# Sparse attention and a maxout layer in one kernel: the list of work units in another order

## The chip, the core and the metric

The kernel runs on one core of one Trainium2 chip. The metric is device time in microseconds. Three runs of the kernel before gave 179.69, 180.04 and 180.06 us, a median of 180.04. One execution was also taken by the hardware profiler; all rows below are from it.

A core has a matrix engine (PE in the profile, its weight loads PEld), a vector engine (DVE), an activation engine (ACT), a general engine (POOL, also called GpSimd) and a queue that issues most transfers (SP). Each takes its own instructions strictly in the order in which they were written; an instruction that has to wait holds up everything behind it on its engine.

## The reference

```python
def _attn_ref(q, k, v, n_global, n_local):          # q, k, v: (4, 8, 768, 64), n_global 8, n_local 96
    scores = scale * np.matmul(q, k.transpose(0, 1, 3, 2))
    rel = pos[:, None] - pos[None, :]
    is_global = pos[None, :] < int(n_global)
    is_local = (rel >= 0) & (rel < int(n_local))
    keep = is_global | is_local
    dist = np.where(is_global & ~is_local, float(n_local), np.abs(rel).astype(np.float32))
    scores = np.where(keep, scores - slopes * dist, -1000000000.0)   # slopes: one per head
    a = softmax(scores)
    return np.matmul(a, v)
...
    x = attn_out.transpose(0, 2, 1, 3).reshape(B * S, H * D)         # (3072, 512)
    h = np.maximum(np.maximum(x @ w1, x @ w2), x @ w3)               # (3072, 768)
    return (h @ w_out)                                               # (3072, 512)
```

Each query sees the first 8 keys of its batch and the last 96 keys up to itself. All inputs are float32 in memory; the kernel multiplies in bfloat16.

## The kernel before

The 3072 tokens are 24 tiles T of 128 tokens, six to a batch. A tile's scores need its own keys, those of the tile before it, and the 8 global keys, which are written over the first 8 key columns of the tile before. The feed-forward part takes the tiles in seven chunks of 4, 2, 2, 4, 4, 4, 4 tiles.

The order of all work is written by hand, as the string SCHEDULE (line 25). Each word is a unit: a letter, its indices, and mostly a last number that picks the engine (0 ACT, 1 DVE, 2 POOL). Line 475 emits the units in the order of the string. Which instruction stands behind which is thus set by the string alone, on every engine and on SP.

The units, by letter:

- **l**, **c**, **x**: the first 12 tiles' q and k come in five groups. `l` loads one part of a group (line 158), `c` casts it to bfloat16 (183), `x` transposes it on PE (239) and copies the result from PSUM (243). In `l2.0` and `l2.1` the parts are q and k of the third group, tiles 4 and 5. Ending 4 in `x` splits the copy between ACT and DVE.
- **L**, **C n.0**, **X**: the same for single tiles from tile 12 on; `X` with ending 4 has a transfer on SP do the transposing (250), with other endings PE (261). **v** loads a tile's values (174), **C n.1** casts them (189).
- **S** scores of four heads and their exponential (283, 288). With ending 1 two more matmuls add the bias (275); otherwise **M** multiplies by a mask afterwards on DVE (307). **K** and **B** prepare masks (300) and biases (295).
- **G** and **V** write the global keys and values into place (214, 216, 221).
- **A** the weighted sum of values (322, 325), then reciprocal and product on DVE (331, 332). **T** transposes the result into the chunk's input: on PE with a copy (349, 350), or with ending 4 by a transfer on SP (340).
- **w**, **W** load and cast w1 to w3 (417, 427); **o**, **Q** the same for w_out (422, 430).
- **F c.f.j** one block of 128 hidden columns of chunk c with weight matrix j: four matmuls (361); j = 0 is copied to SBUF by ACT (366), j = 1 and 2 are maxima on DVE (368, 370). **O** is the product with w_out for a tile (376), its copy (382) and its store (383). **E** is the last chunk's O.
- **D** multiplies zeros on PE (436).

PSUM is tight: the scores and the weighted sums share two buffers, sp0 and sp1 (for `A` the last number picks one); F, O and some transposes share three; one more is for transposes. The raw q/k tiles have five buffers, the raw v tiles six.

Of the kernel before, what the change touches and what calls it, by code (L numbers as in the profile page):

```python
# [22 lines left out]


SCHEDULE = """
    K0 K1 K2 K3 K4 K5 l1.0 l1.1 D0.3 c0.0.2 B0.1 B1.1 B2.1 B3.0 K6 B4.1 B5.1 c0.1.1 c1.0.2 x0.0.4 B6.1
    B7.1 x0.1.4 S0.0.1 v0 l2.0 l2.1 K7 S0.1.1 G0.0 S1.0.1 S1.1.0 x1.0.3 c1.1.2 M0.0 M0.1 M1.0 v1 x1.1.4
    C0.1.2 v2 A0.1 G1.2 S2.0.1 M1.1 c2.0.2 x2.0.1 C1.1.1 S2.1.0 G2.2 S3.0.1 M2.0 M2.1 C2.1.1 T0.1 S3.1.1
    M3.0 M3.1 c2.1.2 v3 A1.0 C3.1.0 w0.0 V1.2 x2.1.2 w1.0 A2.1 V2.2 A3.0 T1.0 T2.1 T3.1 W1.0.1 W0.0.0
    G3.2 S4.0.0 S4.1.0 F0.0.0 F0.1.0 M4.0 F0.2.0 F0.3.0 G4.1 S5.0.0 M4.1 S5.1.0 w0.1 W0.1.1 w0.2 W0.2.2  # L30
    V3.2 F0.0.1 F0.1.1 F0.0.2 F0.1.2 v4 C4.1.0 A4.0 V4.2 w1.1 W1.1.2 W2.0.0 F0.4.0 F0.5.0 M5.0 M5.1 w1.2
    W1.2.2 v5 W2.1.0 T4.0 F0.2.1 F0.3.1 l3.0 l3.2 F0.4.1 l3.1 c3.0.2 c3.2.2 F0.5.1 o2 C5.1.0 A5.1 l3.3
    F0.2.2 Q2.2 F0.3.2 W2.2.0 o0 T5.0 F0.4.2 o1 F0.5.2 x3.0.0 F1.0.0 F1.1.0 c3.1.1 F1.2.0 x3.2.0 Q0.2
    F1.0.1 F1.1.1 F1.2.1 l4.0 l4.1 c3.3.0 F1.0.2 F1.1.2 F1.2.2 x3.1.2 x3.3.1 F1.3.0 F1.4.0 Q1.2 F1.3.1
    S6.0.0 S6.1.0 v6 v7 v8 G6.0 F1.3.2 F1.5.0 v9 c4.0.1 F1.4.1 S7.0.0 S7.1.0 G7.2 v10 M6.0 M6.1 M7.0
    M7.1 O0.0.0 F1.4.2 c4.1.1 C6.1.2 C7.1.2 L12 F1.5.1 S8.0.0 S8.1.0 x4.0.0 O0.1.0 A6.0 x4.1.2 A7.1 V7.2
    F1.5.2 v11 T6.0 O0.2.0 T7.1 G8.2 C8.1.2 S9.0.0 S9.1.0 G9.1 v12 v13 O0.3.0 F2.0.0 F2.1.0 S10.0.0 M8.0
    M8.1 M9.0 M9.1 S10.1.0 C9.1.2 L13 L14 F2.0.1 F2.1.1 F2.0.2 A8.0 C12.0.1 F2.1.2 G10.2 O1.0.0 V8.2
    A9.1 X12.1 M10.0 M10.1 C10.1.0 C11.1.0 F2.2.0 S11.0.0 S11.1.0 M11.0 M11.1 L15 F2.3.0 F2.4.0 O1.1.0
    V9.2 A10.1 F2.2.1 V10.2 T8.0 F2.3.1 F2.5.0 T9.0 A11.1 F2.4.1 T10.0 F2.2.2 F2.3.2 T11.1 F2.4.2  # L40
    S12.0.0 S12.1.0 F2.5.1 C13.0.2 C14.0.2 C15.0.1 X13.4 F3.0.0 F3.1.0 F3.0.1 G12.1 C12.1.0 F3.2.0
    F3.1.1 F3.2.1 S13.0.0 S13.1.0 F2.5.2 v14 C13.1.0 C14.1.2 M12.0 M12.1 F3.0.2 F3.1.2 X14.4 F3.2.2
    X15.4 G13.2 M13.0 M13.1 S14.0.0 S14.1.0 F3.3.0 F3.4.0 F3.5.0 M14.0 M14.1 G14.1 A12.0 A13.1 F3.3.1
    F3.4.1 F3.5.1 S15.0.0 M15.0 S15.1.0 G15.0 v15 V13.2 L16 L17 v16 T12.4 v17 M15.1 O2.0.0 C15.1.0 A14.0
    V14.2 F3.3.2 F3.4.2 T13.4 F3.5.2 C16.1.0 C16.0.2 X16.3 T14.4 C17.0.2 A15.1 X17.4 O2.1.0 S16.0.0
    S16.1.0 G16.1 L18 V15.2 L19 T15.1 M16.0 O3.0.0 M16.1 F4.0.0 F4.1.0 F4.0.1 F4.1.1 C18.0.2 L20 C19.0.2
    A16.1 F4.2.0 F4.3.0 S17.0.0 S17.1.0 F4.2.1 F4.0.2 F4.3.1 v18 M17.0 v19 M17.1 X18.3 X19.4 C20.0.0
    V16.2 F4.1.2 C17.1.2 O3.1.1 A17.1 F4.2.2 F4.3.2 S18.0.0 M18.0 S18.1.0 M18.1 F4.4.0 T16.4 T17.4
    F4.4.1 C18.1.2 C19.1.1 F4.4.2 X20.4 G18.1 S19.0.0 S19.1.0 F4.5.0 L21 M19.0 M19.1 v20 F4.5.1 A18.0
    T18.4 F4.5.2 A19.1 T19.4 V19.1 C21.0.1 X21.4 G19.1 L22 C22.0.2 L23 X22.4 O3.2.1 O3.3.0 O4.0.1  # L50
    S20.0.0 S20.1.0 M20.0 G20.0 O4.1.0 F5.0.0 F5.1.0 F5.2.0 S21.0.0 S21.1.0 G21.2 F5.0.1 F5.1.1 M20.1
    M21.0 F5.3.0 F5.0.2 F5.1.2 F5.2.1 F5.2.2 v21 C20.1.1 C21.1.2 F5.4.0 S22.0.0 M21.1 S22.1.0 C23.0.0
    F5.3.1 M22.0 M22.1 F5.5.0 F5.3.2 A20.0 V20.2 G22.2 v22 F5.4.1 X23.4 v23 F5.5.1 T20.4 A21.1 V21.1
    T21.4 F5.4.2 F5.5.2 S23.0.0 S23.1.0 M23.0 O4.2.0 M23.1 C22.1.2 A22.0 C23.1.0 O4.3.0 V22.2 T22.4
    A23.1 T23.4 O5.0.1 O5.1.0 O5.2.1 O5.3.0 F6.0.0 F6.1.0 F6.0.1 F6.0.2 F6.2.0 F6.3.0 F6.4.0 F6.1.1
    F6.2.1 F6.1.2 F6.3.1 F6.4.1 F6.2.2 F6.3.2 F6.5.0 F6.4.2 F6.5.1 F6.5.2 E
"""


# [1 line left out]
def kernel(  # L61
# [73 lines left out]
    xT = {}  # L135
# [87 lines left out]
    def early(T):  # L223
        return T < NSTART
# [109 lines left out]

    def u_XT(T, how):
        c, i = where[T]
        if i == 0:
            xT[c] = xT_pool.tile([128, NP, len(chunks[c]) * 128], BF16, name="xT", tag="xT")
        if how == 4:
            nc.sync.dma_start_transpose(out=xT[c][:, :, i * 128:(i + 1) * 128],  # L340
                                        in_=xb[T].rearrange("p h d -> p (h d)"))
            return
        if early(T):
            tp = psH.tile([128, NP, 128], BF16, name="xtp", tag="h")
        else:
# [4 lines left out]
        copies[how](xT[c][:, :, i * 128:(i + 1) * 128], tp)  # L350

    ht = {}
    h01s = {}

    def u_F1(c, f, j):
        W = len(chunks[c]) * 128
        if f == 0 and j == 0:
            ht[c] = ht_pool.tile([128, NF, W], BF16, name="ht", tag="ht")
        ps = psH.tile([128, W], FP32, name="h", tag="h")
        for dm in range(4):  # L360
            nc.tensor.matmul(ps, w123[f // 2][:, dm, j, (f % 2) * 128:(f % 2) * 128 + 128],  # L361
                             xT[c][:, dm], start=(dm == 0), stop=(dm == 3))
        if j == 0:
            h01 = h01_pool.tile([128, W], BF16, name="h01", tag="h01")
            h01s[c, f] = h01
            nc.scalar.copy(h01, ps)  # L366
        elif j == 1:
            nc.vector.tensor_max(h01s[c, f], h01s[c, f], ps)  # L368
        else:
            nc.vector.tensor_max(ht[c][:, f], h01s[c, f], ps)  # L370
# [58 lines left out]
    def cast_wo(i, how):  # L429
        copies[how](wo[:, 2 * i:2 * i + 2], wst["o", i])  # L430

    def u_D(i, n):

        wp = psH.tile([128, 512], FP32, name="wp", tag="h")
        for _ in range(n):
            nc.tensor.matmul(wp, zeros[:, 0:128], zeros, start=True, stop=True)

    with tc.manual_schedule():
# [71 lines left out]
```

## Time and profile before

| | |
|---|---|
| median of the runs | 180.04 us |
| profiled execution, first to last instruction (span) | 178.3 us |
| median less span | 1.74 us |
| PE busy | 166.9 us (94%) |
| DVE, ACT, POOL busy | 118.9, 103.1, 37.5 us |
| first matmul of the feed-forward part (F0.0.0) | 23.44 us after the span's start |
| last matmul ends | about 175.05 us |
| moved by transfers | 35.52 MB, mean 199 GB/s |

The page tells of the profiled execution only its span; its own run time is not listed, so the 1.74 us are taken as what lies around the span. Busy time of PE overlaps from one matmul to the next, so a full PE row says that it did not stand idle, and not that each matmul is as short as can be. A landing time below is the start of a transfer's issue on SP plus the time from issue to landing.

### The profile page before, as it was taken

The numbers are of one execution on the slowest core, as the hardware profiler recorded it, in microseconds if no ns is written. First come the engines' busy times: TensorE is split into PE (matmuls) and PEld (weight loads), VectorE is DVE, ScalarE is ACT, GpSimd is POOL, SyncE is SP. The second block draws the span as 40 slices with busy tenths as digits, with TensorE's granted clock in tenths as the row PEclk, the third lists the DMA queues.
The fourth block names the chain that finished last, engine by engine and source line by source line (L and its number), as shares of the span: only waits on it lengthen the run. The fifth ranks groups of instructions, "written<-read, shape, count | busy, mean of one in ns | idle before, by whom it ended". The sixth has DMA issues, their size and how long they took to land.

```text
span 178.3 us, 3960 instructions
## 1 busy us (share of the span) xinstructions
PE 166.9 (94%) x1529; PEld 95.8 (54%) x1551; DVE 118.9 (67%) x237; ACT 103.1 (58%) x160; POOL 37.5 (21%) x65
## 2 busy tenths in 40 slices
PE   3599799999999999999999999999999999999992
PEld 0455644558867677845555555545444555444442
DVE  4519875986787689748979447979358896136620
ACT  4867898646689858555744837351772643341122
POOL 4355203543343112310007024100020401000000
PEclk9999999999999999999999999999999999999998
DMA  5999999999998999989544999769889674610006
GB/s 140 292 271 242 357 320 384 320 361 358 251 193 213 229 254 236 174 171 233 94 90 118 159 247 235 157 132 186 173 153 294 136 143 146 224 42 4 0 11 226
DMA packets 83587, 35.52 MB, mean 199 GB/s; under 512 B 66160, under 2 KB 78320, under 8 KB 83568
## 3 DMA queue, kind: packets, MB, share of 16 engines
q1 hardware_dynamic: 83424, 35.20, 82.8%
q8 instruction: 12, 0.20, 0.5%
q10 hardware_dynamic: 144, 0.07, 0.1%
q14 instruction: 7, 0.06, 0.1%
HBM read 25.17 MB, written 6.29 MB: 176 GB/s over the span
## 4 chain that ended last, share of the span: by engine, by line
PE 85%; DMA 8%; SPq 2%; issue 1%; POOL 1%; DVE 1%; ACT 1%; ACTq 0%
PE h L361 53%; PE po L376 17%; PE sp L283 6%; DMA rawv<-in_v_dram 4%; DMA rawp<-in_q_dram 4%; PE op L322 3%; PE op L325 2%; SPq L174 2%; PE tpp L239 2%; PE xtp L349 1%; SPq L158 1%; POOL qkp L183 1%; PE tp L261 1%; DVE xb L332 0%; ACT va L189 0%
## 5 line engine op out<-in xcount | busy, mean ns | idle before, releaser
L361 PE MATMUL h<-xT,w 128*128 128x512 bf16 (+1 forms) x491 | 99.2, 348 | 0.7 <-issue 0.2
L361 PEld LDWEIGHTS <-w 128*128 128x128 bf16 x504 | 46.9, 98 | 40.5 <-DVE w L427 0.3
L288 ACT ACTIVATE P<-sp 128x1024 bf16<-128x1024 f32 (+1 forms) x48 | 43.4, 955 | 20.6 <-PE sp L283 20.4
L368 DVE TENSOR_TENSOR h<-h,h 128x512 bf16<-128x512 bf16 (+1 forms) x42 | 25.3, 610 | 25.7 <-PE h L361 16.5
L366 ACT CAST h<-h 128x512 bf16<-128x512 f32 (+1 forms) x42 | 21.6, 533 | 21.5 <-PE h L361 21.3
L376 PE MATMUL po<-wo,ht 128*128 128x512 bf16 (+2 forms) x147 | 33.1, 362 | 0.5
L370 DVE TENSOR_TENSOR ht<-h,h 128x512 bf16<-128x512 bf16 (+1 forms) x42 | 25.1, 607 | 3.7 <-PE h L361 3.0
L307 DVE TENSOR_TENSOR P<-P,wmask 128x1024 bf16<-128x1024 bf16 x36 | 24.8, 718 | 3.6 <-ACT P L288 3.5
L376 PEld LDWEIGHTS <-ht 128*128 128x128 bf16 x156 | 14.0, 98 | 13.9
L382 ACT COPY ost<-po 128x512 f32<-128x512 f32 (+2 forms) x20 | 11.2, 564 | 17.8 <-PE po L376 17.7
L332 DVE TENSOR_TENSOR xb<-op,rz 128x512 bf16<-128x512 f32 x24 | 16.6, 692 | 0.8
L283 PEld LDWEIGHTS <-qkT 64*128 64x128 bf16 x352 | 10.2, 96 | 10.0 <-issue 8.0
L283 PE MATMUL sp<-qkT 64*128 64x128 bf16 x352 | 15.2, 223 | 0.4 <-DVE xb L332 0.4
L322 PEld LDWEIGHTS <-P 128*128 128x128 bf16 x192 | 12.5, 97 | 2.5 <-ACT P L288 0.2
L221 POOL COPY va<-vaf 8x260 int32<-8x260 int32 x14 | 6.3, 452 | 34.5 <-PE op L325 34.5
L198 POOL CAST qkb<-raw 128x1024 bf16<-128x1024 f32 x7 | 7.2, 1037 | 27.7 <-DMA raw<-in_q_dram 18.9
L322 PE MATMUL op<-va,P 128*128 128x65 bf16 x160 | 12.3, 193 | 0.7 <-ACT va L189 0.6
L239 PE MATMUL tpp<-identb,qkp 128*128 128x128 bf16 x96 | 8.5, 246 | 4.0 <-POOL qkp L183 3.4
L325 PEld LDWEIGHTS <-P 128*128 128x128 bf16 x160 | 10.4, 97 | 2.2 <-issue 0.7
L239 PEld LDWEIGHTS <-qkp 128*128 128x128 bf16 x96 | 7.0, 111 | 5.8 <-POOL qkp L183 4.3
L325 PE MATMUL op<-va,P 128*128 128x65 bf16 x128 | 9.9, 193 | 0.0
L243 ACT COPY qkT<-tpp 128x1024 bf16<-128x1024 bf16 (+1 forms) x9 | 7.9, 874 | 3.4 <-PE tpp L239 3.4
(66 smaller groups left out, 107.5 us busy)
## 6 DMA issues: line engine op xcount, KB each, us to landing
rawv<-in_v_dram SPq DMA_DIRECT2D x24, 256.0 KB, 4.8
out_dram<-ost SPq DMA_DIRECT2D x23, 256.0 KB, 2.3
rawp<-in_q_dram SPq DMA_DIRECT2D x6, 512.0 KB, 7.2
rawp<-in_k_dram SPq DMA_DIRECT2D x6, 512.0 KB, 7.4
wst<-in_moe_w_dram SPq DMA_DIRECT2D x3, 1024.0 KB, 9.7
raw<-in_q_dram SPq DMA_DIRECT2D x12, 256.0 KB, 4.1
raw<-in_k_dram SPq DMA_DIRECT2D x12, 256.0 KB, 4.8
wst<-in_moe_w_dram SPq DMA_DIRECT2D x3, 512.0 KB, 8.7
```

Source lines behind the costliest of these rows:

```text
L239: nc.tensor.transpose(tp[:, e, j - lo], qb["p", n, s][:, e, 2 * j:2 * j + 2].rearrange("i h d -> i (h d)"), identb)
L283: nc.tensor.matmul(sp[:, hh, j2, ds], qT(T - ds, 1)[hsl, jp], qT(T, 0)[hsl, jp], start=not how, stop=True, skip_group_check=True)
L288: nc.scalar.activation(P[:, :, 0:n], sp.rearrange("p a b d n -> p (a b) d n")[:, :, 0:n], AF.Exp, bias=0.0, scale=scale)
L307: nc.vector.tensor_mul(P, P, wmask[:, g, :, 0:2])
L322: nc.tensor.matmul(o, P[:, i, 0], heads(va[T])[:, h], start=True, stop=(t == 0), skip_group_check=True)
L325: nc.tensor.matmul(o, P[:, i, 1], heads(va[T - 1])[:, h], start=False, stop=True, skip_group_check=True)
L332: nc.vector.tensor_tensor(out=x.rearrange("p (g h) d -> p g h d", g=2), in0=o4[:, :, :, 0:64], in1=rz[:, :, :, None].to_broadcast([128, 2, ...
L361: nc.tensor.matmul(ps, w123[f // 2][:, dm, j, (f % 2) * 128:(f % 2) * 128 + 128], xT[c][:, dm], start=(dm == 0), stop=(dm == 3))
L366: nc.scalar.copy(h01, ps)
L368: nc.vector.tensor_max(h01s[c, f], h01s[c, f], ps)
L370: nc.vector.tensor_max(ht[c][:, f], h01s[c, f], ps)
L376: nc.tensor.matmul(po, ht[c][:, f, tt * 128:(tt + 1) * 128], wo[:, f, cols], start=(f == 0), stop=(f == NF - 1))
```

## The change

Nothing that is computed changes, except that one more or one fewer unit takes the bias way instead of the mask way. What changes is the string, and with it three things in the functions: a chunk's tiles `xT` and `ht` are now made by whichever unit of the chunk comes first (before, by the first index), and D may be called with a count of nothing, in which case it does nothing.

The start of the string, before and after:

```diff
-    K0 K1 K2 K3 K4 K5 l1.0 l1.1 D0.3 c0.0.2 B0.1 B1.1 B2.1 B3.0 K6 B4.1 B5.1 c0.1.1 c1.0.2 x0.0.4 B6.1
-    B7.1 x0.1.4 S0.0.1 v0 l2.0 l2.1 K7 S0.1.1 G0.0 S1.0.1 S1.1.0 x1.0.3 c1.1.2 M0.0 M0.1 M1.0 v1 x1.1.4
-    C0.1.2 v2 A0.1 G1.2 S2.0.1 M1.1 c2.0.2 x2.0.1 C1.1.1 S2.1.0 G2.2 S3.0.1 M2.0 M2.1 C2.1.1 T0.1 S3.1.1
-    M3.0 M3.1 c2.1.2 v3 A1.0 C3.1.0 w0.0 V1.2 x2.1.2 w1.0 A2.1 V2.2 A3.0 T1.0 T2.1 T3.1 W1.0.1 W0.0.0
-    G3.2 S4.0.0 S4.1.0 F0.0.0 F0.1.0 M4.0 F0.2.0 F0.3.0 G4.1 S5.0.0 M4.1 S5.1.0 w0.1 W0.1.1 w0.2 W0.2.2
...
+    K4 B2.1 K0 D3.4 K7 B3.2 K3 B1.1 D1.4 D0.2 l1.0 B0.1 K6 K1 K2 c0.0.2 B5.2 x0.0.2 c0.1.1 x0.1.4 K5
+    S0.0.1 l1.1 c1.1.1 B7.2 B4.2 B6.2 S1.1.0 c1.0.2 v0 M0.0 G0.1 C0.1.2 S1.0.0 G1.2 x1.0.3 S0.1.1
+    M0.1 x1.1.0 A0.1 M1.0 S2.0.1 M1.1 S2.1.1 v1 T0.1 l2.0 c2.0.1 G2.2 S3.0.0 v3 v2 C2.1.1 M3.0
+    S3.1.1 C3.1.0 l2.1 C1.1.2 A1.0 G3.1 M3.1 V1.2 M2.1 M2.0 A2.1 V2.2 x2.0.0 w0.0 W0.0.2 c2.1.1 A3.0
+    T2.0 x2.1.4 T1.1 T3.0 S4.0.0 M4.0 w1.0 W2.0.1 S4.1.0 D4.1 F0.0.0 G4.2 F0.1.0 S5.0.0 S5.1.0 w0.1
+    W0.1.1 F0.4.0 w0.2 M5.0 V3.2 F0.5.0 v4 w1.1 W1.1.0 F0.1.1 v5 M4.1 F0.0.1 W1.0.2 W0.2.2 F0.1.2
+    F0.0.2 C4.1.2 A4.0 C5.1.1 W2.1.2 F0.3.0 F0.2.0 M5.1 F0.2.1 w1.2 W2.2.0 T4.1 V4.2 A5.0 F0.5.1
...
```

On SP the first transfers after the second group go from `v0 l2.0 l2.1 v1 v2 v3` to `v0 v1 l2.0 v3 v2 l2.1`, and `w1.2 v5` becomes `v5 w1.2`. The fourth group and what follows go from `l3.0 l3.2 l3.1 o2 l3.3 o0 o1 l4.0 l4.1 v6` to `l3.3 l3.2 l3.0 l3.1 v7 l4.1 o0 v6 o1 l4.0 o2`. The string keeps its later stages in the same broad order; within each the units are shuffled, and casts and small copies change engine. Over the whole string, by count: zero matmuls 3 to 11; score units with bias 6 to 5; T units by a transfer 11 to 13 (tiles 8 and 9 are added); bias units on POOL 0 to 5; casts of w_out on ACT 0 to 2 (all three were on POOL); casts of w1 to w3 on POOL 3 to 5; casts of v on DVE 4 to 9.

The functions:

```diff
@@ u_XT
-        if i == 0:
+        if c not in xT:
             xT[c] = xT_pool.tile([128, NP, len(chunks[c]) * 128], BF16, name="xT", tag="xT")
@@ u_F1
-        if f == 0 and j == 0:
+        if c not in ht:
             ht[c] = ht_pool.tile([128, NF, W], BF16, name="ht", tag="ht")
@@ u_D
-    def u_D(i, n):
+    def u_D(i, n=0):
+        if n == 0:
+            return
```

More of the change, by code (lines that the diff above doesn't have):

```diff
@@ L31 @@
[L31 to L55, printed above, removed]
@@ L56 @@
-    F6.2.1 F6.1.2 F6.3.1 F6.4.1 F6.2.2 F6.3.2 F6.5.0 F6.4.2 F6.5.1 F6.5.2 E
+    K4 B2.1 K0 D3.4 K7 B3.2 K3 B1.1 D1.4 D0.2 l1.0 B0.1 K6 K1 K2 c0.0.2 B5.2 x0.0.2 c0.1.1 x0.1.4 K5
[3 more added lines that the diff above has]
+    T2.0 x2.1.4 T1.1 T3.0 S4.0.0 M4.0 w1.0 W2.0.1 S4.1.0 D4.1 F0.0.0 G4.2 F0.1.0 S5.0.0 S5.1.0 w0.1
@@ new lines @@
+    W0.1.1 F0.4.0 w0.2 M5.0 V3.2 F0.5.0 v4 w1.1 W1.1.0 F0.1.1 v5 M4.1 F0.0.1 W1.0.2 W0.2.2 F0.1.2
+    F0.0.2 C4.1.2 A4.0 C5.1.1 W2.1.2 F0.3.0 F0.2.0 M5.1 F0.2.1 w1.2 W2.2.0 T4.1 V4.2 A5.0 F0.5.1
+    F0.4.1 T5.0 l3.3 W1.2.2 F0.3.1 F0.2.2 F0.4.2 l3.2 c3.2.2 c3.3.0 x3.3.4 F0.5.2 F1.3.0 x3.2.0
+    F1.0.0 l3.0 c3.0.2 G6.1 F1.0.1 F1.1.0 x3.0.1 l3.1 c3.1.2 x3.1.2 v7 F0.3.2 F1.0.2 S6.1.0 l4.1 o0
+    v6 C6.1.2 S6.0.0 M6.0 M6.1 F1.5.0 F1.5.1 Q0.0 o1 l4.0 S7.1.0 S7.0.0 F1.1.1 F1.1.2 F1.3.1 F1.5.2
+    F1.2.0 A6.1 F1.4.0 F1.2.1 M7.1 G7.2 S8.0.0 S8.1.0 F1.3.2 c4.1.2 x4.1.3 o2 Q2.0 F1.4.1 v9 F1.2.2
@@ new lines @@
+    G8.2 Q1.2 C9.1.1 T6.1 v8 S9.1.0 S9.0.0 F1.4.2 M8.1 M7.0 C7.1.1 L13 L12 v10 v11 G9.1 O0.0.0
+    c4.0.2 O1.0.0 L14 A7.1 x4.0.0 O0.3.0 v15 S10.0.0 C8.1.1 M8.0 S10.1.0 T7.1 M9.0 C12.0.1 M9.1
+    M10.0 O0.1.0 v13 V7.2 A8.0 T8.4 V8.2 O0.2.0 F2.5.0 F2.5.1 C10.1.1 F2.3.0 C13.0.2 X13.4 A9.0 T9.4
+    V9.0 F2.5.2 F2.2.0 G10.1 M10.1 F2.4.0 X12.3 F2.4.1 A10.1 V10.1 F2.3.1 L15 C11.1.2 C14.0.2 F2.3.2
+    G12.1 X14.4 S11.0.0 S11.1.0 L18 F2.1.0 v12 O1.1.0 T10.0 F2.0.0 M11.0 C13.1.1 M11.1 F2.2.1 A11.0
+    F2.4.2 F2.1.1 F2.1.2 T11.1 F2.2.2 F2.0.1 S13.1.0 S13.0.0 M13.0 C15.0.1 G13.2 F3.1.0 F3.1.1
@@ new lines @@
+    S12.1.0 S12.0.0 F3.0.0 C15.1.0 F3.3.0 X15.4 F2.0.2 M13.1 S14.0.0 S14.1.0 G14.1 L16 v14 v18
+    F3.3.1 F3.3.2 F3.1.2 M14.1 C18.0.2 X18.0 O2.0.0 L19 C12.1.2 A13.0 F3.0.1 V13.2 F3.5.0 M12.0
+    M12.1 F3.5.1 M14.0 v16 S15.0.0 L21 S15.1.0 F3.4.0 C14.1.2 F3.2.0 G15.0 A14.0 T14.4 T13.4 A12.1
+    F3.2.1 V14.1 T12.4 F3.2.2 M15.1 L17 C16.0.2 X16.1 C19.0.0 C18.1.0 X19.4 F3.5.2 S18.0.0 S18.1.0
+    F3.4.1 M18.0 F3.0.2 L20 v17 F3.4.2 S16.1.0 S16.0.0 M15.0 C21.0.2 C17.0.2 X17.4 G16.2 G18.1
+    O3.0.0 v19 A15.1 O3.3.1 T15.0 O2.1.0 F4.2.0 F4.1.0 M16.1 M18.1 C20.0.3 X20.4 A18.1 L22 F4.3.0
@@ new lines @@
+    F4.5.0 M16.0 F4.1.1 V15.1 S19.0.0 S19.1.0 G19.0 C16.1.1 F4.1.2 F4.3.1 S17.0.0 S17.1.0 C17.1.1
+    O3.1.1 M17.1 F4.2.1 A16.1 C19.1.0 F4.5.1 F4.2.2 F4.3.2 v20 T18.4 X21.4 M19.0 S20.0.0 M19.1 M20.0
+    V16.2 S20.1.0 F4.4.0 M17.0 T16.4 L23 F4.0.0 F4.0.1 F4.4.1 A19.1 A17.0 C22.0.0 X22.4 M20.1 F4.5.2
+    F4.0.2 T19.4 T17.4 C20.1.2 G20.2 S21.0.0 S21.1.0 v21 O3.2.1 V19.2 C23.0.0 X23.4 F4.4.2 v22 A20.1
+    O4.2.1 v23 G21.2 S22.0.0 C22.1.2 M22.0 S22.1.0 M21.1 M22.1 F5.1.0 F5.2.0 F5.2.1 F5.4.0 G22.0
@@ L57 @@
+    C21.1.0 F5.0.0 M21.0 V20.0 F5.0.1 S23.1.0 S23.0.0 M23.0 F5.2.2 T20.4 O4.0.0 M23.1 F5.5.0 A21.1
+    T21.4 F5.0.2 F5.4.1 F5.3.0 V21.2 A22.0 C23.1.2 T22.4 O4.3.0 V22.2 A23.0 T23.4 F5.1.1 F5.5.1
+    F5.1.2 O4.1.0 F5.3.1 F5.3.2 F5.4.2 F6.2.0 F5.5.2 F6.3.0 F6.1.0 F6.1.1 F6.4.0 O5.0.0 O5.1.0
+    F6.3.1 F6.1.2 F6.3.2 F6.2.1 F6.2.2 F6.0.0 O5.2.1 F6.0.1 O5.3.0 F6.0.2 F6.4.1 F6.4.2 F6.5.0
+    F6.5.1 F6.5.2 E D2.0
 """
```

## The prediction

> **What bounds the kernel now.** I read the busy shares first, then the slices, then the chain that ended last for the first 24 us, then single rows of ACT, PE and POOL.
>
> ```profile
> PE 166.9 (94%) x1529; PEld 95.8 (54%) x1551; DVE 118.9 (67%) x237; ACT 103.1 (58%) x160; POOL 37.5 (21%) x65
> ...
> PE   3599799999999999999999999999999999999992
> ...
> DMA  5999999999998999989544999769889674610006
> ```
>
> From the sixth slice on PE is full, and until 85 us so are the transfers. DVE, ACT and POOL have room. The early chain:
>
> ```profile
> 9.61 0.43 SPq L158
> 10.05 0.04 issue
> 10.09 1.17 SPq L174
> 11.26 0.04 issue
> 11.30 1.73 SPq L174
> 13.03 0.04 issue
> 13.07 7.08 DMA rawv<-in_v_dram
> 20.16 0.02 issue
> 20.18 0.63 ACT va L189
> 20.81 0.04 issue
> 20.85 0.19 PE op L322
> ```
>
> The values of tile 3 (v3), issued last of the ten early loads, land at 20.16; their cast, A3, its product on DVE and T3 follow, and the feed-forward part starts at 23.44. ACT casts its first weights just before:
>
> ```profile
> 22.24 1.05 ACT L427 CAST w<-wst 128x1024 bf16<-128x1024 f32 x1
> ```
>
> So there are two stages: up to 23.44 us landings decide, from there to 175.05 PE's own work does. To see that this second stage hides no waits I added up its work from the rows: 360 matmuls of 512 columns at 0.2158 (F0, F3 to F6) 77.7; 144 of 256 at 0.109 15.7; w_out 144 at 0.2158 31.1; S 9.8 (0.275 a unit, 0.165 for a batch's first tile); A 8.9 (0.48 and 0.24); nine T at 0.22 2.0; transposes of q and k 9 at 0.45 4.05. That is 149.2 of the 151.6 that pass. Of the other 2.4 about 1.2 are the pauses of 0.05 called "issue", and the rest lies spread over some 150 units. There is nearly no wait to win there, and any new wait is lost in full.
>
> Two rows matter further down:
>
> ```profile
> 10.27 1.03 PE L275 MATMUL sp<-bias,identb 128*128 128x512 bf16 x2
> 14.14 0.59 PE L275 MATMUL sp<-bias,identb 128*128 128x512 bf16 x2
> ...
> 50.87 0.81 POOL L189 CAST vaf<-rawv 128x512 bf16<-128x512 f32 x1
> 51.62 1.07 POOL L189 CAST va<-rawv 128x512 bf16<-128x512 f32 x1
> ```
>
> The same pair of matmuls takes half the time at 14 us that it took at 10. And POOL's cast of v, mostly 0.61, took up to 1.07.
>
> **The change part by part.**
>
> *Zero matmuls, 10 instead of 3 ahead of the first transposes.* Three took 1.46, so ten take about 4.4, from 1.19 to 5.6; the first transposes start at 6.08, when their cast is done. They lie in idle time: nothing. If they warm PE as its busy time by 14 us seems to have, the transposes and scores between 6 and 13 us get about 2.5 us shorter, but what ends the stage are landings at 16 to 22, so nothing again. One more (D4.1, 0.22) stands before F0.0.0, inside the wait below.
>
> *The ten early loads.* They carry 4.2 MB in both orders, and before they landed in order of issue: v0 11.5, l2.0 13.3, l2.1 15.15, v1 16.4, v2 18.0, v3 20.16; then w0.0 21.7, w1.0 24.4. By bytes ahead of it, in the new order v3 lands near 15.2, v2 near 16.4 (where v1 did), and l2.1 last: SP issues it near 12.9 and it needs 6.7 to 7.1, so 19.8. The weights keep their place.
>
> *The path to F0.0.0 now.* DVE takes, in this order: cast of v2 (16.4 to 16.8), mask of S3.0 (0.69), product of A1 and of A2 (0.9 each, to about 19.5), then the cast of l2.1, 0.69, which waits for 19.8: 20.5. Behind it stand the product of A3 (0.91, 21.4), DVE's half of the copy of x2.1 (0.68, 22.1) and T1's copy (0.42, 22.5). F0.0.0 needs that copy. It also needs the cast of w0.0, now on POOL: 21.7 + 1.04 = 22.75, and POOL has nothing else then. The later decides: F0.0.0 at 22.85 instead of 23.44, **-0.6**. With l2.1 late this becomes landing + 2.85. The moved casts (B to POOL, two group casts to DVE) lie earlier: B on POOL I cost at 0.45, between DVE's 0.35 and POOL's 1.04 for a cast of 1024, nearest to its 0.61 for 512; four of them, 1.8, fit between the casts at 6.0 and 8.5, and with 1.04 each the second group's cast ends at 11.2 instead of 9.6, before its copy's turn behind the next cast on DVE (11.1).
>
> *Weights behind that.* W2.0 is ready on DVE at 24.4 + 0.7 = 25.1; PE needs it after two F (0.863 each) and S5 (0.55), at 25.1. w1.2 goes behind v5 on SP: landing 34.1 becomes 35.0, its cast on POOL ends at 36.1, and by the list PE needs it at 36.9. Covers of 0 to 0.8 us: nothing if they hold, else each us late counts.
>
> *T8 and T9 by a transfer.* Two units of 0.22 leave PE's full stage: **-0.44**, with the copies (0.5 each) off ACT. SP gets two issues of about 1.25 each; behind them on SP stand a store and the loads of tiles 15 and 18, whose casts come 7 and 13 us of PE's work later, and F3 needs the result 10 us later. Hidden.
>
> *One bias unit less.* S in the early stage loses 0.43 on PE, DVE gains a mask of 0.7; both before 23.44. Nothing.
>
> *w_out's loads go behind v7, l4.1, v6, l4.0.* o2 landed at 41.1; by bytes it now lands at 50.9 (l4.1 landed at 48.9 with the same loads but v7 and v6, at 1.0 each). Its cast, 1.05 on ACT, ends at 52.0; O0.0.0, which needs all three, comes to PE at 22.85 + 30.0 = 52.9. Cover 0.9.
>
> *The shuffle of the rest.* By PE's work between units: S to A is at least 2.8 us in both orders, reuse of sp0 and sp1 at least 1.15 (before 1.16; needed: an exponential of 1.03, or DVE's 0.9, and a hop). The tightest now: S8.1 1.15 after A6; O3.0.0 0.55 after the last F3, whose maximum DVE still owes, with four matmuls (0.86) of cover; and some 9 us in the fourth chunk where DVE has 9.6 us to do in PE's 9.2. None must cost; each can cost 0 to 0.4, up to 0.8 in all. I take **+0.2**, near the lower end, since before, spaced alike, lost almost nothing.
>
> **Sum.** -0.6 - 0.44 + 0.2 = -0.84: a span of 177.5 against the profiled 178.3. The median of the runs, 180.04, lies 1.74 above that span, and I carry that over: **179.2 us**.
>
> **A rule that speaks against it.** POOL's cast of 1.07 us began at 51.62, while DVE multiplied two SBUF operands (the masks); elsewhere it took 0.61. That is 0.46 lost. If it also strikes the two casts on POOL that PE waits for, w0.0 (+0.46) and w0.2 (28.45 against a need at 28.6: +0.3), the sum is -0.84 + 0.76 = -0.1, 179.95 us, which is rival 2. The Trainium skill (GPSIMD Engine Reference, Specifications) says that GpSimd shares its SBUF interfaces with VectorE and contends with DVE instructions that have two SBUF inputs; by that rule POOL casts beside masks are stretched, and those two rows agree. Against the rival: between 21.7 and 22.75 DVE's items read PSUM.
>
> **The rivals.**
>
> 1. *The start does not move.* If l2.1 lands at 20.5, or another load takes the place of the one removed, F0.0.0 stays at 23.4 and only T8, T9 and the small waits count: -0.24, 179.8. For it: ten loads of the same bytes end at the same time, whatever their order.
> 2. *POOL stretched*, as above: 179.95.
> 3. *The third group's k comes with the weights* (slower). In DVE's list its cast stands ahead of A3's product and T1's copy. If l2.1 shares the engines with w0.0, issued right behind it, and lands with it at 21.7, F0.0.0 is at 24.55, +1.1, and with -0.24 the sum is +0.87: 180.9. It ends slower from a landing at 21.2 on. For it: 512 KB at the tail, where v3 with half the bytes took 7.08; against: every load before landed in order.
> 4. *PE waits for w_out* (slower). If v7 and v6 delay o2 to 54 (their issues on SP took 1.78 each instead of 1.0, and ACT, blocked by that cast, holds the exponentials of tile 9), O0.0.0 waits until 55.1, +2.2: 181.4. It decides from 53.1 on. Against: it asks for 3 us.
>
> **How the numbers follow.** Forecast 0.56; rival 1 0.08, rival 2 0.08, rival 3 0.15, rival 4 together with other waits of its size 0.13. Less than 0.2% (0.36 us) is about what a measurement of this kernel cannot tell from no change. The forecast's own range is 178.7 to 179.7: down to -1.3 with no small wait and a start some 0.25 earlier (w0.0 landing that much before 21.7), up to -0.3 with 0.8 of small waits. That upper edge and rivals 1 (-0.24) and 2 (-0.1) are within 0.36: same 0.02 + 0.16 = 0.18, faster 0.54, slower 0.28. The range for eight in ten goes from 178.6 (the forecast's end, and 0.1 for the scatter of the runs) to 181.1 (rival 3 and 0.2), leaving out rival 4.
>
> **What would show it.** The start: PE's first matmul of line 363 near 22.85, with POOL's cast of w before it. DVE idle before the cast of the third group, until a landing near 19.8. The zero matmuls: ten, and the pair of bias matmuls in 0.6 from the first. T on PE 11 units instead of 13. A PE row without idle from the sixth slice on, and little idle in PE's rows of w_out near 53. The prediction is wrong if l2.1 lands after 21, if PE stands between 45 and 55, or if the full stage takes longer than 151.5 from first to last matmul.

## The result: slower by 3.9%, and the profile after

The four runs of the changed kernel took 185.78, 188.43, 189.08 and 190.61 us (median 188.75), where those of the kernel before lay between 179.69 and 180.21 (median 180.05). Ratios, here and below, leave out runs more than 1.5% above the fastest of their kernel: here 189.08 and 190.61, further down one of 184.32 and two of about 289.9 at half clock from end to end. The other two have a mean of 187.1, 7.1 above before: a ratio of 1.0394, 95% interval 1.0318 to 1.0471. The prediction said 179.2, and its range ended at 181.1. The profiled execution is that of 189.08, with a span of 187.2 us against 178.3, so what is added up from its rows below is more than 7.1. The string is two lines longer, so line numbers behind it are two higher than before, and four behind the function of the zero matmuls (a bias unit is line 297 instead of 295).

From the page, the busy time of the engines, then the rows of PE, of POOL and of PE's granted clock in 40 slices of 4.68 us:

```profile
PE 170.2 (91%) x1528; PEld 96.7 (52%) x1549; DVE 127.7 (68%) x240; ACT 101.8 (54%) x154; POOL 43.0 (23%) x67
...
PE   7639786999999969998999999999999999999992
...
POOL 6981445260143060004040231002000200000000
PEclk9987999999999996999999999999999999999999
```

Before, PE's row was full from the sixth slice on. Now it has a hole in the third slice, a smaller one in the seventh and another in the fifteenth, the clock falls behind the first and the last, and POOL is busy nine tenths of the second slice. What POOL does there is in its timeline (start, length, engine and line, operation, count, and in brackets the idle time before it with what ended it):

```profile
3.82 1.42 POOL L297 TENSOR_SCALAR bias<-rbase 128x384 bf16<-128x384 f32 x1 [0.75 <-DVE rbase L474]
5.19 1.03 POOL L185 CAST qkp<-rawp 128x1024 bf16<-128x1024 f32 x1
6.19 5.58 POOL L297 TENSOR_SCALAR bias<-rbase 128x384 bf16<-128x384 f32 x4
11.83 1.04 POOL L185 CAST qkp<-rawp 128x1024 bf16<-128x1024 f32 x1
```

The same instruction by shape, on POOL after and on DVE before (busy us, mean ns of one):

```profile
L297 POOL TENSOR_SCALAR bias<-rbase 128x384 bf16<-128x384 f32 x5 | 6.8, 1362 | 0.9 <-DVE rbase L474 0.8
```

```profile
L295 DVE TENSOR_SCALAR bias<-rbase 128x384 bf16<-128x384 f32 x7 | 2.1, 354 | 0.0
```

One bias unit takes 1.36 on average on POOL and 0.35 on DVE. The second group's q is cast behind the four, at 11.83 to 12.87; before, that cast ended at 9.6. PE waits for it, and the rest of the start moves with it. PE's timeline:

```profile
12.92 1.04 PE L241 MATMUL tpp<-identb,qkp 128*128 128x128 bf16 x8 [2.93 <-POOL qkp L185]
...
26.04 1.89 PE L363 MATMUL h<-xT,w 128*128 128x512 bf16 x7
...
30.04 4.27 PE L363 MATMUL h<-xT,w 128*128 128x512 bf16 x19 [1.56 <-DVE w L429]
```

F0.0.0 is at 26.04 instead of 23.44 (forecast: 22.85). Four microseconds later PE waits another 1.56, for a weight that DVE casts. DVE's rows there, and 39 us later:

```profile
26.87 2.10 DVE L309 TENSOR_TENSOR P<-P,wmask 128x1024 bf16<-128x1024 bf16 x1 [1.11 <-ACT P L290]
28.89 1.70 DVE L429 CAST w<-wst 128x1024 bf16<-128x1024 f32 x2
...
65.71 4.02 DVE L309 TENSOR_TENSOR P<-P,wmask 128x1024 bf16<-128x1024 bf16 x2
```

and POOL's in the same two places:

```profile
26.40 2.02 POOL L429 CAST w<-wst 128x1024 bf16<-128x1024 f32 x2
...
66.61 1.03 POOL L200 CAST qkb<-raw 128x1024 bf16<-128x1024 f32 x1
67.60 0.61 POOL L191 CAST va<-rawv 128x512 bf16<-128x512 f32 x1
68.15 1.03 POOL L200 CAST qkb<-raw 128x1024 bf16<-128x1024 f32 x1
```

A mask takes 0.69 alone. Beside two casts of POOL without a gap between them it takes 2.10; the second mask of the last DVE row takes 3.415, beside a train of three (casts that run back to back). PE runs dry, and then runs at half its clock (busy time and granted clock of PE in windows of 2 us):

```profile
68.00:70.00 2.00, 0.52 (x5) 1.00 0.68 164
70.00:72.00 2.00, 1.37 (x19) 0.67 0.06 12
72.00:74.00 2.00, 2.00 (x11) 0.50 0.76 203
```

The 8.9 us of span, added up: F0.0.0 later 2.6; the wait for the weight 1.56; idle time of PE between 60 and 90 us 3.2 against 0.3 before (8.46, 9.32 and 9.05 busy of ten each, against 9.89, 9.95 and 9.90), so 2.9; half clock, 0.33 of 1.37 and 0.50 of 2.00, so 1.45. Together 8.5. (The windows go by the clock and do not hold the same units in both kernels, so this is a rough account.) The rest is a few tenths in each of several places.

### The profile page after: what moved, and what is told of

Read it like the earlier page. It is cut to its first block, busy times and chain, and to the rows that moved or that the text cites. A ratio compares the mean times of both kernels' runs of the same rounds, so it can differ in the third digit from the quotient of the medians.

```text
span 187.2 us, 3953 instructions
## 1 busy us (share of the span) xinstructions
PE 170.2 (91%) x1528; PEld 96.7 (52%) x1549; DVE 127.7 (68%) x240; ACT 101.8 (54%) x154; POOL 43.0 (23%) x67
## 4 chain that ended last, share of the span: by engine, by line
PE 78%; DVE 8%; POOL 6%; ACT 3%; issue 2%; POOLq 0%; ACTq 0%
PE h L363 47%; PE po L378 15%; PE sp L285 6%; POOL bias L297 4%; DVE P L309 4%; PE tpp L241 3%; PE op L324 3%; PE op L327 2%; ACT P L290 2%; PE xtp L351 1%; POOL qkp L185 1%; DVE qkb L200 1%; DVE xb L334 1%; DVE h L370 1%; DVE qkp L185 1%
## 5 line engine op out<-in xcount | busy, mean ns | idle before, releaser
L363 PE MATMUL h<-xT,w 128*128 128x512 bf16 (+1 forms) x489 | 101.4, 352 | 3.2 <-DVE w L429 1.6
L363 PEld LDWEIGHTS <-w 128*128 128x128 bf16 x504 | 47.4, 99 | 43.8 <-DVE w L429 1.7
L378 PE MATMUL po<-wo,ht 128*128 128x512 bf16 (+2 forms) x150 | 33.6, 362 | 0.4
L309 DVE TENSOR_TENSOR P<-P,wmask 128x1024 bf16<-128x1024 bf16 x37 | 29.8, 824 | 5.5 <-ACT P L290 5.5
L324 PEld LDWEIGHTS <-P 128*128 128x128 bf16 x192 | 12.8, 100 | 4.7 <-DVE xb L334 2.4
L324 PE MATMUL op<-va,P 128*128 128x65 bf16 x160 | 12.8, 195 | 2.6 <-DVE xb L334 2.1
L223 POOL COPY va<-vaf 8x260 int32<-8x260 int32 x11 | 4.6, 422 | 35.7 <-PE op L327 28.2
L241 PE MATMUL tpp<-identb,qkp 128*128 128x128 bf16 x96 | 8.0, 235 | 4.8 <-POOL qkp L185 3.6
L327 PEld LDWEIGHTS <-P 128*128 128x128 bf16 x160 | 10.8, 99 | 1.8 <-issue 0.5
L327 PE MATMUL op<-va,P 128*128 128x65 bf16 x128 | 10.3, 196 | 0.0
L333 DVE RECIPROCAL rz<-op 128x8 f32<-128x8 f32 x24 | 4.9, 204 | 7.7 <-PE op L327 6.1
L200 POOL CAST qkb<-raw 128x1024 bf16<-128x1024 f32 x6 | 6.6, 1104 | 14.5 <-DMA raw<-in_k_dram 8.4
```

Of the source, the lines that this page charges most:

```text
L241: nc.tensor.transpose(tp[:, e, j - lo], qb["p", n, s][:, e, 2 * j:2 * j + 2].rearrange("i h d -> i (h d)"), identb)
L309: nc.vector.tensor_mul(P, P, wmask[:, g, :, 0:2])
L324: nc.tensor.matmul(o, P[:, i, 0], heads(va[T])[:, h], start=True, stop=(t == 0), skip_group_check=True)
L327: nc.tensor.matmul(o, P[:, i, 1], heads(va[T - 1])[:, h], start=False, stop=True, skip_group_check=True)
L378: nc.tensor.matmul(po, ht[c][:, f, tt * 128:(tt + 1) * 128], wo[:, f, cols], start=(f == 0), stop=(f == NF - 1))
```

## The experiments

**The five bias units on DVE.** The changed kernel with one thing undone; the five stand on DVE directly behind its other three:

```diff
- K4 B2.1 K0 D3.4 K7 B3.2 K3 B1.1 D1.4 D0.2 l1.0 B0.1 K6 K1 K2 c0.0.2 B5.2 x0.0.2 c0.1.1 x0.1.4 K5
- S0.0.1 l1.1 c1.1.1 B7.2 B4.2 B6.2 S1.1.0 ...
+ K4 B2.1 K0 D3.4 K7 K3 B1.1 D1.4 D0.2 l1.0 B0.1 B3.1 B5.1 B7.1 B4.1 B6.1 K6 K1 K2 c0.0.2 x0.0.2 ...
+ S0.0.1 l1.1 c1.1.1 S1.1.0 ...
```

> The changed kernel with its five POOL bias units on DVE again, between 4.9 and 6.4 us where DVE stands idle; all else as changed. Theory P (GpSimd): a bias unit takes 1.4 us on POOL, five of them held the cast of the second group until 11.83 instead of 8.5, and the feed-forward part started at 26.04. Expected: that cast at 8.6, F0.0.0 at 22 to 23, the run 3 to 4 us below the changed kernel's 188.75, if the later waits stay as they are. Rival D (transfers): the landings of the reordered loads set the start; then F0.0.0 stays within 0.5 of 26.0 and the time within 1 us of 188.75.

Measured: 180.68 us (180.64 to 180.84), ratio to before 1.004 (1.0025 to 1.0055), span 179.0. Of the 7.1 us lost, 6.4 come back; the expectation had 3 to 4. The scatter goes too: these four runs lie within 0.2, those of the changed kernel within 4.8. DVE's eight bias units, and PE's first feed-forward matmuls:

```profile
3.70 3.08 DVE L297 TENSOR_SCALAR bias<-rbase 128x384 bf16<-128x384 f32 x8
```

```profile
23.03 1.89 PE L363 MATMUL h<-xT,w 128*128 128x512 bf16 x8
```

Three microseconds of that are the start itself (26.04 to 23.03). The rest (5.2 between the two profiled executions, 3.4 by the means) comes back mostly because a later start also moves POOL's casts: here W1.0 and W0.2 wait for their landings one by one, where in the changed kernel they run back to back (the row at 26.40) and a mask falls into them. POOL's rows in this run:

```profile
24.48 1.57 POOL L429 CAST w<-wst 128x1024 bf16<-128x1024 f32 x1 [1.04 <-DMA wst<-in_moe_w_dram]
...
27.50 1.04 POOL L429 CAST w<-wst 128x1024 bf16<-128x1024 f32 x1 [1.45 <-DMA wst<-in_moe_w_dram]
...
63.98 1.11 POOL L200 CAST qkb<-raw 128x1024 bf16<-128x1024 f32 x1 [0.33 <-DMA raw<-in_k_dram]
```

One train is left in this kernel, near 62 us, so that one does not come from the late start but from the list itself. Its last cast waits 0.33 for a landing, and the mask gets through in this gap, after 2.43 and not 3.415. From the view of the mask's tile the shortest, median and longest duration in ns:

```profile
L309 DVE TENSOR_TENSOR P<-P,wmask x2: 685/1558/2431, 61.2 to 61.8; 128x1024 bf16<-128x1024 bf16 x2
```

**Fewer casts on POOL, bias units left there.** Four casts that stood in or beside trains go to ACT:

```diff
- ... W1.0.2 W0.2.2 F0.1.2 ...   C13.0.2 ...   C11.1.2 C14.0.2
+ ... F0.5.0 W0.2.0 v4 ...       C13.0.0 ...   C11.1.0 C14.0.0
```

> The changed kernel with four casts taken off POOL and put on ACT (the second block of w1, the q/k of tiles 13 and 14, the values of tile 11), so that no three POOL casts stand back to back beside masks; bias units stay on POOL. Theory P: the masks of DVE (two SBUF operands) wait for a POOL cast and for each that follows without a gap; the 4.02 us for two masks at 65.7 becomes 1.3 and the 2.10 at 26.9 becomes about 1, PE's idle 1.6 near 29 and 2.5 near 69 go, and with them its half clock near 72: 4 to 5 us below 188.75. Rival O (the shuffle as such, many small waits): less than 1.5 us.

Measured: 184.05 us (183.06 to 184.44), ratio 1.0233 (1.0214 to 1.0251). That is 4.7 below the median that the expectation names and 3.1 below the mean of 187.1, with the start still late, at 25.95:

```profile
28.55 2.76 PE L363 MATMUL h<-xT,w 128*128 128x512 bf16 x12 [0.16 <-DVE w L429]
```

The wait of 1.56 for the weight is 0.16, and PE is full from 60 to 70 us. A mask takes 704 ns on average (824 in the changed kernel, 718 before). So the trains are a second loss beside the start, of 3.1 of the 7.1.

**Both.**

> Both edits together. Theory P: 179.5 to 182. Rival O: above 184, as the waits move elsewhere.

Measured: 180.28 us (180.07 to 180.96), ratio 1.0018 (1.0008 to 1.0027), span 178.7. This is not the sum of the two (6.4 and 3.1 would be more than the 7.1 lost): with the start repaired one train is gone already. It has a stall of its own, since W0.2 on ACT comes behind exponentials:

```profile
29.49 1.68 PE L363 MATMUL h<-xT,w 128*128 128x512 bf16 x7 [0.41 <-ACT w L429]
```

**One part alone, on the kernel before.** Five bias units on POOL, at their old places in the string, and nothing else:

```diff
- ... B2.1 B3.0 K6 B4.1 B5.1 c0.1.1 c1.0.2 x0.0.4 B6.1 B7.1 ...
+ ... B2.1 B3.2 K6 B4.2 B5.2 c0.1.1 c1.0.2 x0.0.4 B6.2 B7.2 ...
```

> The kernel before with one part of the change alone: the bias units B3 (ScalarE), B4, B5, B6 and B7 (VectorE) on GpSimd, at their old places in the list. Theory (1.17 to 1.6 us a unit on GpSimd): three of them stand between its casts of the first group, two behind the second; its third cast ends near 15 instead of 11.4, the feed-forward part starts 1.5 to 3.6 later than 23.4, and the time is 181.5 to 183.6, more if delayed casts then run in trains beside masks. Rival (the prediction's 0.45 a unit, or 1.04 without loss): 180.0.

Measured: 185.89 us (185.69 to 186.22), ratio 1.0325 (1.0311 to 1.0338). POOL's rows, then PE's first feed-forward matmul, then two of PE's waits (total, times, longest), then the masks of DVE between 36 and 41 us:

```profile
5.99 3.87 POOL L295 TENSOR_SCALAR bias<-rbase 128x384 bf16<-128x384 f32 x3
9.81 1.03 POOL L183 CAST qkp<-rawp 128x1024 bf16<-128x1024 f32 x1
10.92 2.41 POOL L295 TENSOR_SCALAR bias<-rbase 128x384 bf16<-128x384 f32 x2
```

```profile
27.08 3.61 PE L361 MATMUL h<-xT,w 128*128 128x512 bf16 x15
```

```profile
PE sp L275 <- POOL bias L295: 3.5, 2, 2.6
PE h L361 <- DVE h L368: 1.7, 1, 1.7
```

```profile
L307 DVE TENSOR_TENSOR P<-P,wmask x2: 677/2328/3980, 36.3 to 40.2; 128x1024 bf16<-128x1024 bf16 x2
```

The five units (1.25 each here) move F0.0.0 by 3.64: PE waits 3.5 for the last two themselves, as its score matmuls add those biases. Behind that a mask waits 3.98 through four casts of POOL in a row and PE 1.7 for what DVE does after it. The move alone, without any other part of the change, costs more (5.9) than the direct delay, by the same second loss. It went 2.3 beyond the upper end of the expectation, which had named the trains but given them no price.

**What two engines do to each other.** A kernel of its own, which computes nothing of the task and writes zeros: eight instructions on DVE beside 0 to 4 casts on POOL, then each alone.

> A kernel that computes nothing of the task: it only runs DVE operations beside 0 to 4 POOL casts of 128x1024 back to back, stage by stage, and writes zeros. Theory P: a DVE product of two bfloat16 SBUF operands (0.69 alone) that starts during n casts of 1.04 ends only when the last of them does, so that one of the eight takes up to 1.7, 2.7, 3.8 and 4.8 us for n of 1 to 4; a maximum with one PSUM operand and a copy out of PSUM keep their 0.42; the plain cast of a float32 SBUF tensor waits as the product does. POOL's casts stay at 1.04. The bias operation alone on POOL takes 1.2 to 1.4. Rival: POOL is the one that waits (as its 1.07 for a cast of 0.61 in the kernel before suggests): then the products stay at 0.69 and the casts stretch.

DVE's rows: products of two bf16 SBUF operands beside no cast, beside three; plain casts in SBUF beside three; products with one PSUM operand beside three. Then POOL's: three casts beside the products, three beside the PSUM products, four casts alone, four of the bias instruction alone.

```profile
8.87 5.77 DVE L59 TENSOR_TENSOR dq<-dq,mask 128x1024 bf16<-128x1024 bf16 x8
...
28.69 8.05 DVE L59 TENSOR_TENSOR dq<-dq,mask 128x1024 bf16<-128x1024 bf16 x8
...
45.52 8.05 DVE L62 CAST dq<-rawb 128x1024 bf16<-128x1024 f32 x8
...
53.56 5.73 DVE L65 TENSOR_TENSOR dq<-dq,pt 128x512 bf16<-128x512 bf16 x8
```

```profile
29.37 3.92 POOL L77 CAST pq<-raw 128x1024 bf16<-128x1024 f32 x3
...
53.85 3.00 POOL L77 CAST pq<-raw 128x1024 bf16<-128x1024 f32 x3
...
70.75 3.98 POOL L77 CAST pq<-raw 128x1024 bf16<-128x1024 f32 x4
...
75.35 4.58 POOL L80 TENSOR_SCALAR pq<-raw 128x384 bf16<-128x384 f32 x4
```

Each cast of POOL costs the eight products 0.7 to 0.85 (6.62, 7.33, 8.05, 8.77 beside one to four), and each product in turn costs POOL about half a microsecond. It is the same for a plain cast from SBUF to SBUF, and nothing for a DVE instruction with a PSUM operand. The bias instruction takes 1.15 on POOL with nobody beside it: most of its 1.36 is POOL's own price. The rest is contention: of the four in a row in the changed kernel two take 1.17, and the two with a cast of DVE beside them (at 6.79 and at 10.44) 1.62 and 1.41. The expectation that one product would wait for the whole train failed here: the engines took turns.

**One product, released while POOL's casts run.**

> Nothing of the task is computed: zeros are written. ScalarE's copy (about 1 us) releases products of two bf16 operands (128x1024) on VectorE while GpSimd is in the first of 0 to 4 back-to-back casts of 1024; stages of one product, then of two and of four. Theory (an engine that waits for the other has its turn when the running instruction ends, as in the eight products beside casts: 1.49 us a pair): one product takes 0.69 alone and at most 0.69 and the rest of one cast, so up to 1.7, with any number of casts. Rival (a product that begins while a cast runs is passed over until the casts are through): 1.7 or less with one cast, 2.7 with two, 3.7 with three, 4.7 with four, as the masks of 2.10 beside two and 3.4 beside three suggest; and the second product of a stage takes 0.69.

The product beside four casts (beside two and three it is the same 1.49), and the four casts:

```profile
21.13 1.49 DVE L71 TENSOR_TENSOR dq<-dq,mask 128x1024 bf16<-128x1024 bf16 x1 [1.26 <-ACT dq L69]
```

```profile
20.05 4.44 POOL L60 CAST pq<-raw 128x1024 bf16<-128x1024 f32 x4
```

With two casts or more it is always 1.49: one cast, then its turn (0.69 beside none or one, which was over by then). The product started near the boundary between the first and the second cast, not in the middle of one.

**The same with the kernel's operands, and with loads in flight.**

> Nothing of the task is computed: zeros are written. One product on VectorE, released by ScalarE while GpSimd is in the first of three or four back-to-back casts, as before (there it took 1.49 with any number of casts), now with the operands of the kernel: the mask as a view of four pieces of 256 out of 384 columns, the cast's output in four pieces of 256; and then the same with loads from HBM in flight. Theory (the turn goes to the waiting engine whatever the operands): 1.5 in all stages, and the masks of 2.1 to 4.0 in the kernel come from something that no run shows. Rival A (operands in pieces make the product lose its turn): 1.5 in the plain stage and 2.7 to 3.7 in those with the view or with pieces. Rival B (loads in flight do it): 1.5 without and 2.7 to 3.7 with them.

Between 1.49 and 1.55 in all stages with casts, so both rivals fall. With the view as operand, the cast's output in pieces and loads from HBM running:

```profile
39.34 1.55 DVE L74 TENSOR_TENSOR dq<-dq,wmask 128x1024 bf16<-128x1024 bf16 x1 [1.21 <-ACT dq L95]
```

Why masks of the real kernel were passed over for 2.1 to 4.0 us while a product alone never waited for more than one cast is open. Those masks began in the middle of an instruction of POOL, and these products near the boundary of one. That is not what decides, as another mask of the changed kernel shows. It begins 0.15 inside a cast, another cast of POOL follows without a gap, and it has its turn after the first (the second takes 1.07 instead of 0.61):

```profile
85.19 1.43 DVE L309 TENSOR_TENSOR P<-P,wmask 128x1024 bf16<-128x1024 bf16 x1 [1.60 <-ACT P L290]
```

```profile
85.04 1.04 POOL L200 CAST qkb<-raw 128x1024 bf16<-128x1024 f32 x1 [1.47 <-DMA raw<-in_k_dram]
86.03 1.07 POOL L191 CAST vaf<-rawv 128x512 bf16<-128x512 f32 x1
```

**A better base: bias units on DVE, and three casts on ACT.** The first experiment's edit, with C13.0, C11.1 and C14.0 on ACT and W0.2 left on POOL.

> The changed kernel with the five bias units on VectorE and three of its casts of q and k (C13.0, C11.1, C14.0) on ScalarE; the cast W0.2 stays on GpSimd. Theory (trains of GpSimd casts beside masks cost what is left after the bias units): the run with both earlier edits took 180.28 and lost 0.57 to W0.2 on ScalarE (the lag of PE by 30 us was 0.77 against 0.20), so 179.7, and PE full between 60 and 70 us. If nothing but the five bias units and that train went wrong, the forecast itself: 179.2. Rival (the rest comes from the new order as a whole, whatever engine casts): 180.6, as with the bias units moved alone.

Measured: 179.49 to 180.78 us, ratio 0.9994 (0.9978 to 1.0009), so no difference from before. The eleven times lie in two groups, six from 179.49 to 179.72 and five from 180.30 to 180.78. The theory's 179.7 is their median, 179.72, but it lies at the edge of a group and not in the middle of one. No profile of this kernel is used below; starts are compared with the next one's.

**Three zero matmuls instead of eleven**, on that base (`D3.4`, `D1.4`, `D4.1` out, `D0.2` to `D0.3`).

> The kernel of this call with five bias units on VectorE and three casts on ScalarE, but three zero matmuls in one place instead of ten in four. Theory: landings set the start, so F0.0.0 stays within 0.1 of where it is and the time within 0.3 us. Rival (they keep TensorE's clock up, and the scores of the first groups end later without them): the pairs of bias matmuls by 10 us take 1.03 instead of about 0.6, F0.0.0 comes up to 0.5 later and the time is up to 0.5 longer. Second rival (the zero matmul just ahead of F0.0.0 is in the way): 0.2 shorter.

The prose of the expectation counts ten in four places; with the one ahead of F0.0.0 it is eleven. Measured: 179.49 to 180.75, ratio 1.0004 (0.999 to 1.0018): nothing. The profiled execution (179.54, span 177.8) is of the lower group. PE's rows:

```profile
10.60 1.03 PE L241 MATMUL tpp<-identb,qkp 128*128 128x128 bf16 x8
...
22.92 1.89 PE L363 MATMUL h<-xT,w 128*128 128x512 bf16 x8
```

Such eight transposes at 10 us took 0.62 in the runs of the first and the third experiment, which have eleven zero matmuls, but 0.93 to 1.03 in the three runs that follow below, which have eleven too (in the first two of these the granted clock is at 0.50 from 9 us on). So these profiles do not settle whether the zero matmuls speed up the first groups. In this run it makes no difference to the start: the chain that ends in F0.0.0 goes through the landing of l2.1 at 20.2, and not through PE's work ahead of it.

**T8 and T9 on PE again**, on the same base: `T8.4` and `T9.4` out, `T8.0` behind F2.5.0, `T9.0` behind F2.2.0.

> The same base, but T8 and T9 on TensorE with copies on ScalarE instead of by a transfer. Theory: two units of 0.22 more in a full stage, 0.44 us longer. Rival (TensorE has small waits there which swallow them): 0. Second rival (ScalarE's two copies of 0.5 delay exponentials): 0.9 longer.

Measured: 181.28 us (181.25 to 181.37), ratio 1.0066 (1.0053 to 1.0079): 1.56 above the base's 179.72. 0.44 is the work. Another 0.46 is a wait of T8, since the product that it needs is not there at the place that I gave it:

```profile
63.47 0.40 PE L351 MATMUL xtp<-identb,xb 128*128 128x128 bf16 x4 [0.46 <-DVE xb L334]
```

The last 0.66 is not located; it is less than the distance of the base's two groups.

**The old order of the early loads**, on the same base (`v0 l2.0 l2.1 v1 v2 v3`, all else left).

> The same base, but the early loads in the order of before (v0, q and k of the third group, v1, v2, v3), with the units on the engines left as they are. Theory: v3 lands near 20.2 and v2 near 18.0 instead of 17.0, F0.0.0 comes 0.4 to 0.8 later, and the time is as much longer. Rival (the start does not move, since ten loads of the same bytes end at the same time): 0.

Measured: 180.72 us (four runs 180.67 to 181.96), ratio 1.0051 (1.0029 to 1.0072), about 1.0 above the base.

```profile
23.64 1.89 PE L363 MATMUL h<-xT,w 128*128 128x512 bf16 x8
26.60 4.71 PE L363 MATMUL h<-xT,w 128*128 128x512 bf16 x21 [0.51 <-DVE w L429]
```

The start is 0.72 later than in the run before, in the middle of the expected 0.4 to 0.8, and the chain that ends there goes through v3's landing at 20.1, as in the kernel before. So the new order of the early loads is worth about what was forecast (0.6), as far as one profile of each can tell: the next run, with the new order, starts at 23.33, and then it is 0.3. A wait of 0.51 for the weight W2.0 comes on top.

**Where the two groups of times come from.** W1.0 goes to DVE:

```diff
- w1.0 W2.0.1 S4.1.0 ... F0.0.1 W1.0.2 W0.2.2
+ w1.0 W2.0.1 W1.0.1 S4.1.0 ... F0.0.1 W0.2.2
```

> The base of the last call (five bias units on VectorE, C13.0, C11.1 and C14.0 on ScalarE) and one cast more taken from GpSimd: W1.0 goes behind W2.0 on VectorE, where that engine idles from 25.1 to 25.9. The base's times fell into two groups 0.9 us apart, 179.5 and 180.4. Theory: W1.0 on GpSimd and W2.0 on VectorE are released by the same landing (24.42), and which of the two casts gets through first differs from run to run; when it is GpSimd's, W2.0 is up to 0.7 late and TensorE, which has no cover there, waits. Then all runs now lie near 179.5 (179.3 to 179.8), the span 177.8. Rival (the two groups come from somewhere else): they stay, 0.9 apart.

Measured: 179.68 to 181.25, ratio 1.001 (0.9995 to 1.0025). The theory fails: the scatter stays, now without a gap between groups. The profiled execution was the slowest of the twelve, span 179.5, and shows two places, a start that is 0.4 later and a stop of PE that nothing in the profile explains:

```profile
23.33 1.89 PE L363 MATMUL h<-xT,w 128*128 128x512 bf16 x7
...
128.13 4.05 PE L363 MATMUL h<-xT,w 128*128 128x512 bf16 x18 [0.79 <-issue]
```

At the start, DVE's cast of the third group's k begins at 20.59 instead of 20.26, behind a product that is late. The chain that ends in F0.0.0 runs through the work of DVE, PE and ACT from 4.9 us on, and not through a landing: the eight transposes at 10.60 and the next eight at 12.32 took 1.03 each, where in the run with three zero matmuls the second eight took 0.62. So the start is not always set by landings; why PE was slower there is open, as the profile shows its clock as 1.00. What the 0.79 is stays open too. No version tried beats the kernel before by more than the measurement can tell.

## Why the prediction was wrong, point by point

**The step that failed** is "B on POOL I cost at 0.45, between DVE's 0.35 and POOL's 1.04 for a cast of 1024, nearest to its 0.61 for 512". It measured 1.36. The rows that I took were of another instruction: POOL needs 1.0 for a cast of 1024 columns, but for a TENSOR_SCALAR of 384 it needs 1.15 alone and up to 1.62 in the chain. By column that is three times as much, so 1.04 was no upper bound either. Four units between two casts are 5.58 and not "1.8", and the fifth stands ahead of the first cast. With the measured price the prediction's own sum shows the delay: the second group's cast ends at 12.87, where its sentence had "11.2" as the worst case, still in time for the copy.

**What followed from it was not in the sum at all.** A start that is 2.6 late should cost 2.6. With the bias units back on DVE 6.4 us came back, since the list was tight further on: casts that had been spread out by their landings ran in trains, masks stood behind them, PE dried out and lost its clock. About 1 us more belongs to the list alone, in the train near 62 us that is there with the start on time. The step "The shuffle of the rest", "each can cost 0 to 0.4, up to 0.8 in all", holds only for a list that runs on time.

**The rival "POOL stretched" had the right contact and the wrong direction.** It has POOL's casts stretched by 0.46. That happens (26.40 to 28.42 was followed by a cast of 512 that took 1.04 instead of 0.61), but the dear case is DVE's masks waiting, 2.10 and 3.415, and behind them the W cast that PE needs. The Trainium skill (SBUF — State Buffer, section "SBUF: two separate sides") says more than the page that I had cited: the port pair of the two engines is locked for a whole instruction, and the other one blocks fully. The runs agree that the two exclude each other (PSUM operands are free), though not quite for the whole of both: a pair takes 1.49, less than 0.69 and 1.0 together. A mask that is passed over four times in a row is not in it.

**Zero matmuls: nothing.** Right for the time (medians of 179.88 and 179.72 with three and with eleven, less apart than the runs of either). The reason given, that landings end the stage, holds in the profile with three and not in that of the last experiment.

**The early loads.** v3 landed near 15.9 and v2 near 17.0 (forecast 15.2 and 16.4), l2.1 near 20.2 in most repaired kernels and near 18.7 in the changed one and in the last experiment (forecast 19.8). F0.0.0 came at 22.92 to 23.33 in the repaired kernels, against 22.85. The mechanism was right and the size about right, and the old order on the same base is 0.3 to 0.7 later. Rivals 1 and 3 did not happen.

**Weights behind that.** Covers of 0 held in the repaired kernels and not in the changed one, where W2.0, at 28.89, was late by a mask.

**w_out.** The late start of the changed kernel tests nothing here, as O0.0.0 comes only at 58.27. In the kernel with three zero matmuls the last cast of w_out ends at 53.35 and O0.0.0 begins at 53.68, with PE busy throughout. Right, with a cover of 0.33 and not 0.9; rival 4 did not happen.

**T8 and T9.** The sign was right, the size is not clean: 1.56 with a wait of my own making in it.

**The small waits: +0.2.** Mis-sized. In the best profiled run of the repaired kernel it is 154.9 us from F0.0.0 to the end, exactly as long as before (178.3 less 23.44); with T8 and T9 gone by 0.44, the small waits are thus about 0.44 there and not 0.2, and in about half of the runs 0.9 more. So even with the bias units on DVE and that train removed the forecast's 179.2 is not reached: 179.5 at best, 179.7 in the median.

## What to carry to other kernels

A unit that is moved to another engine is priced by a row of that very operation on that engine, or bounded by the worst row per element times a few; a cast of another size is no bound for it. Where a list of work is tight, an early delay of 2.6 us can cost more than twice that, so price what the delayed engine's queue will then do back to back, and who shares a port with it. Repairing the first cause brought back nearly all of it (6.4 of 7.1); repairing the consequences alone brought 3.1.

## What the runs showed of the hardware

- TENSOR_SCALAR from f32 to bf16, 128x384: 1.15 alone and on average 1.25 and 1.36 in two kernels on POOL, 0.35 on DVE. The Trainium skill (GPSIMD Engine Reference, section 4.1) calls elementwise work with one input roughly line-rate there; this row differs, and the measurement decides.
- POOL's cast of 1024 columns holds up DVE's products of two SBUF operands and its plain casts in SBUF (0.7 to 0.85 per cast), and leaves DVE's instructions with a PSUM operand alone (5.73 for eight, with POOL at 3.00 for three).
- A mask can be passed over by two, three and four casts of POOL (2.10, 3.415, 3.98), though a product alone took its turn after one (1.49), and so did other masks (1.43).
- After about 2 us without matmuls (68.5 to 70.6) PE's granted clock went to 0.50 and stayed there until about 74 us. After a stop of about 1.5 us (28.5 to 30.0) it stayed at 1.00.
